# K products of a chunk in two groups, every other U of the first second stage in the ring of the spatial sums, and another order of the work

## The chip, the cores and the metric

The kernel runs on one core of a Trainium2 chip. A core has five engines, each with its own queue, which it works through in order: PE (TensorE, matmuls; its weight loads are shown apart as PEld), DVE (VectorE), ACT (ScalarE), POOL (GpSimd) and SP (SyncE, which here only issues transfers). The metric is the device time of one execution in microseconds (us). Before the change it is 365.99 us, the median of 8 runs (363.04 to 366.72).

## What is computed

Two branches work on the same input `x` of 2048 rows and 640 columns, and a gate mixes them:

```python
g = sigmoid((x * gate_w).sum(-1, keepdims=True))
# branch a: a long convolution along the rows, one filter of length 2048 per column
K = einsum('dn,dnl,dn->dl', C, exp(dt*A * l), dt*B).real      # d 640, n 128, l 2048
a = causal_convolution(K, x) + x * Dskip                       # by FFT in the reference
# branch b: a gated MLP with a product along the rows
z  = gelu(x @ w_in);  z1 = z[:, :864];  z2 = layernorm(z[:, 864:])
b  = (z1 * (w_sp @ z2 + b_sp[:, None])) @ w_out                # w_sp is 2048 x 2048
out = g * a + (1 - g) * b
```

All data are bf16; sums are kept in fp32.

## The kernel before

**Branch b.** `z2_tile` (matmuls at L606) makes z2, sixteen tiles of 128 rows. `z1_tile` (L638) makes z1 in four groups of rows and sends it to memory. `sp_block` is the product along the rows, in eight blocks `tb` of 256 output rows. In a block, 7 tiles of the 864 columns times 16 row tiles of z2 give 112 matmuls of 256 columns (L826, "spatial sums", into `ps_g`), 896 in all. They come in groups of two column tiles, so 32 matmuls fill one `ps_g` (the last group of a block has 16). VectorE adds the bias (L830) and multiplies by z1 (L832), which gives `vT`. Then 28 matmuls of 320 columns (L846, `ps_o`) multiply by `w_out`, 224 in all, and VectorE or ScalarE scales them into `ob` or, for the last four row tiles, `acc`.

**Branch a.** The filter K is made in eight chunks `c` of 80 columns; chunks 0 to 5 belong to the first part (`h` = 0, 480 columns), 6 and 7 to the second (`h` = 1, 160 columns). `k_tables` (L1001) makes tables of cosines, sines and exponentials in `ET`, kept twice, on VectorE, ScalarE and GpSimd. Its last step is the multiply at L1042. `k_sub` (L1048) multiplies the tables: 160 small matmuls a chunk (L1059 and L1060, 80 each, with 32 weight columns and 33 moving columns) into `ps_k`, a pair of PSUM banks. A copy moves it to `kf` (L1068, L1070). `k_store` sends kf to memory, `k_expand` reads it back spread out (`xk`). The convolution then goes by a transform in two stages. `s1_u` (L665, L669) is the first stage for the input, `conv_s1` (L1148, `ps_s1k`) that for the filter; both go through memory (`FU_d`, `FK_d`). `conv_s2` (L1169) is the second stage. For each of 32 indices k, a matmul makes U from `fu` (L1195, `ps_u`), ScalarE copies it to `us`, two matmuls make the filter's side from `fk` (L1202, `ps_s2k`), VectorE multiplies both into `p` (L1204), two matmuls transform back (L1210, `ps_v`), and ScalarE copies to `vs` (L1212). For the second part two indices are done at once, so there are 16 steps. `conv_vt` transposes `vs` on VectorE (L1218, twelve for the first part, four for the second), and `conv_i2` (L1290, L1292) is the last transform, added to branch b's result with the gate (L1226, L1243, L1245).

**PSUM.** Its eight banks are three rings: `two`, two pairs of banks, for `ps_z`, `ps_k`, `ps_s`, `ps_s1k`, `ps_s2k` and `ps_i`; `g`, two banks, for `ps_g` and for `ps_u` of the second part; `x`, two banks, for `ps_o`, `ps_v` and, in the first part, `ps_u`.

**What sets the order.** The program is a list of tasks, each with engines that may do it, a cost, what it reads and writes, and the rings it takes a buffer of. A planner (`Plan`, L139 to L331) plays the tasks through in time when the program is built: whenever an engine is free it takes, among its ready tasks with free buffers, the one with the longest chain of costs behind it plus a `bias`. Where a task may go to several engines, the one that is free takes it. The order so found is written out as the engines' queues. `TUNE` (L38) adds values to the bias of tasks named by function and line, some for one index only. A `lag` makes a task wait in the plan for some time after another; it makes no wait on the chip.

The lines that the change touches:

```python
        tab_ids.append(add("PE", 3.65, m, r=tabs + (["cva"] if h else []), w=[ps], bias=8000, lag=[(tab_ids[-1], 4.0)] if tab_ids else []))
        ...
        i_ = add(("ACT", "DVE"), (0.9, 0.91), ev, r=[ps], w=[(kf, s)], bias=8500)
        ...
            pu = gps("ps_u", [P, 512]) if h else xps("ps_u", [P, 512])
```

So the 160 matmuls of a chunk are one task, with nothing between them on TensorE.

Of the kernel before, what the change touches and what calls it, by code (L numbers as in the profile page):

```python
# [25 lines left out]
class Handle:  # L26
# [12 lines left out]
    ('conv_i2', 37, None): -4167,  # L39
    ('conv_s1', 15, ('g', 0)): -3985,  # L40
    ('conv_s1', 15, ('g', 1)): -4925,
    ('conv_s2', 35, ('h', 0)): 11440,
    ('conv_s2', 27, None): -2461,
    ('conv_s2', 10, None): 1034,
    ('conv_s2', 14, ('h', 0)): 1039,
    ('eights', 13, None): -327,
    ('i2_out', 7, None): -2142,
    ('k_expand', 28, None): -762,
    ('k_exps', 7, ('c', 0)): 1891,
    ('k_exps', 7, ('c', 4)): 2617,  # L50
    ('k_store', 13, ('h', 0)): -14806,
    ('k_store', 13, None): 22358,
    ('k_store', 14, ('h', 0)): 19878,
    ('k_store', 14, ('h', 1)): -1401,
    ('k_sub', 23, ('h', 1)): -10879,
    ('k_sub', 13, ('h', 0)): -8414,
    ('k_sub', 13, None): 1899,
    ('k_tables', 32, ('c', 3)): -2944,
    ('k_tables', 32, None): -581,
    ('k_tables', 41, None): 3697,  # L60
    ('k_tables', 30, ('c', 0)): -3593,
    ('k_tables', 30, ('c', 5)): -5856,
    ('k_tables', 29, None): -22708,
    ('k_tables', 6, ('c', 4)): 86,
    ('k_tables', 6, ('c', 5)): -857,
    ('k_tables', 18, ('c', 7)): 624,
    ('k_tables', 17, ('c', 6)): -17233,
    ('k_tables', 36, ('c', 0)): -6475,
    ('k_tables', 36, ('c', 5)): 223,
    ('k_tables', 36, ('c', 6)): -314,  # L70
    ('k_tables', 36, None): -460,
    ('k_tables', 20, None): -7652,
    ('k_tables', 21, ('c', 2)): 26183,
    ('k_tables', 21, ('c', 3)): 3768,
    ('k_tables', 21, None): -11620,
    ('main', 160, None): 8664,
    ('main', 151, ('g', 0)): 9963,
    ('main', 151, None): 1256,
    ('main', 149, None): 8266,
    ('main', 353, None): -19029,  # L80
    ('main', 370, None): -7683,
    ('main', 369, None): 304,
    ('main', 365, None): -1890,
    ('main', 438, None): 3692,
    ('main', 435, None): 82,
    ('main', 415, None): -970,
    ('main', 443, None): 5378,
    ('main', 421, None): 5294,
    ('main', 424, None): -198,
    ('ob_load', 7, None): 1449,  # L90
    ('quads', 6, None): -6309,
    ('s1_u', 13, ('h', 1)): 12507,
    ('s1_u', 13, ('n0', 12)): 8594,
    ('s1_u', 16, ('h', 1)): -18248,
    ('s1_u', 16, None): 3525,
    ('s1_u', 3, None): -3769,
    ('s1_u', 18, ('h', 1)): -8047,
    ('s1_u', 18, ('n0', 0)): 8453,
    ('s1_u', 14, ('h', 1)): -1860,
    ('s1_u', 14, ('n0', 6)): -9520,  # L100
    ('s1_u', 14, None): -5630,
    ('sp_block', 23, ('tb', 2)): 1896,
    ('sp_block', 23, ('tb', 7)): 872,
    ('sp_block', 25, None): 5230,
    ('sp_block', 20, ('tb', 0)): 7827,
    ('sp_block', 20, ('tb', 5)): -2187,
    ('sp_block', 20, ('tb', 6)): -2437,
    ('sp_block', 20, ('tb', 7)): -5504,
    ('sp_block', 20, None): -13871,
    ('sp_block', 41, None): 1955,  # L110
    ('sp_block', 42, ('tb', 0)): -7911,
    ('sp_block', 42, None): -1644,
    ('sp_block', 47, None): -33736,
    ('sp_block', 3, ('tb', 0)): 1637,
    ('sp_block', 3, ('tb', 4)): -553,
    ('sp_block', 8, ('tb', 0)): 580,
    ('sp_block', 8, ('tb', 1)): -2903,
    ('sp_block', 8, None): -115,
    ('sp_block', 6, ('tb', 0)): 8562,
    ('sp_block', 6, ('tb', 1)): 15972,  # L120
    ('sp_block', 6, None): -8530,
    ('sp_block', 5, ('tb', 7)): 4722,
    ('sp_block', 5, None): -667,
    ('tg_build', 15, None): 5531,
    ('tg_build', 9, None): 7974,
    ('x_group', 3, ('g', 0)): -1676,
    ('x_group', 3, ('g', 1)): -3059,
    ('z1_tile', 17, None): -290,
    ('z1_tile', 10, ('g', 0)): 3083,
    ('z1_tile', 10, ('g', 3)): -2857,  # L130
    ('z1_tile', 15, None): -1480,
    ('z2_tile', 19, None): 222,
    ('z2_tile', 18, None): 422,
    ('z2_tile', 10, None): -1879,
# [200 lines left out]
def kernel(  # L335
# [20 lines left out]
    P = 128  # L356
# [691 lines left out]
    def k_sub(h, s, kf):  # L1048
# [4 lines left out]
        def m(e):  # L1053
            ET, M2, E2 = X["ET", z], X["M2", z], X["E2", z]
            for i in range(SQ):
                for q in range(4):
                    d = SQ * q + i
                    o_ = ps()[32 * q:32 * q + 32, i // 10, 33 * (i % 10):33 * (i % 10) + 33]
                    pe.matmul(o_, lhsT=ET[:, 0:32, d], rhs=M2[:, :, d], start=True, stop=False, tile_position=(0, 32 * q))  # L1059
                    pe.matmul(o_, lhsT=ET[:, NA:NA + 32, d], rhs=E2[:, :, d], start=False, stop=True, tile_position=(0, 32 * q))  # L1060
        tab_ids.append(add("PE", 3.65, m, r=tabs + (["cva"] if h else []), w=[ps], bias=8000, lag=[(tab_ids[-1], 4.0)] if tab_ids else []))
# [327 lines left out]
```

## Time and profile before

| | us |
|---|---|
| median of 8 runs | 365.99 |
| the profiled execution, device time | 365.95 |
| its span, first to last instruction | 364.1 |
| TensorE busy | 316.0 |
| VectorE busy | 286.8 |
| ScalarE busy | 244.2 |
| GpSimd busy | 151.8 |

The mean clock that TensorE was granted is 0.947 of full speed. The span goes through these points: the first K chunk starts at 106.2 us and the eighth ends at 241.9; the first `ps_s2k` runs at 265.7; VectorE's transposes of the first part start at 312.6; the last instruction on VectorE is at 360.

How to read it: "busy" is the time in which an engine's instructions run, without waiting for one another. A timeline row gives start and length in us, engine, line, operation, output and inputs with their shapes, and how many instructions are merged; a bracket at its end is the time in which the engine sat idle before it, and what ended that. In a row of groups, the two numbers after the bar are busy us and mean ns of one; after the second bar stands the idle time of the engine just before the group's instructions, by releaser. The clock row (PEclk) has 40 slices of the span, each a digit in tenths, 9 for 0.9 and more.

### The profile page before, as it was taken

Reading aid. Unit: us, or ns where it says so; the run is one execution under the profiler, and the core shown is the slowest. Engines: PE = TensorE matmul, PEld = TensorE weight load, DVE = VectorE, ACT = ScalarE, POOL = GpSimd, SP = SyncE. Lnnn points to the kernel's source line nnn. Section 1 sums busy time; section 2 is a strip of 40 time slices with the busy share of each in tenths; the row PEclk is TensorE's granted clock in tenths of the full one; section 3 lists DMA queues with packets and bytes.
Section 4 is the critical chain, followed back from the end, with each engine's and each line's share of the span. In section 5 each row is a group of like instructions: output and inputs, shape, how many; then the busy total and the mean of one; then the engine's idle time right before and its main releaser. Section 6 shows DMA issues by size and latency. Waiting matters only on the chain.

```text
span 364.1 us, 8397 instructions
## 1 busy us (share of the span) xinstructions
PE 316.0 (87%) x3237; PEld 221.2 (61%) x3237; DVE 286.8 (79%) x548; ACT 244.2 (67%) x438; POOL 151.8 (42%) x143
## 2 busy tenths in 40 slices
PE   3899999997799999999798979879999999829963
PEld 3455455775485677787685668657755564516741
DVE  4059997887889589896898289727898989996984
ACT  1877757999785756899677368615467778605832
POOL 3004537600668068500899469826483000303111
PEclk9999999999899989999989899969999999967995
DMA  7989887585654569348395577977556767552403
GB/s 200 221 125 223 185 214 217 157 206 149 156 147 133 149 131 233 115 78 251 77 153 99 99 184 177 257 209 195 182 170 179 227 192 204 153 171 99 137 27 99
DMA packets 108085, 59.89 MB, mean 164 GB/s; under 512 B 75918, under 2 KB 104354, under 8 KB 108046
## 3 DMA queue, kind: packets, MB, share of 16 engines
q1 hardware_dynamic: 105662, 54.06, 59.2%
q0 software_dynamic: 2384, 5.30, 5.9%
q8 instruction: 25, 0.41, 0.5%
q14 instruction: 14, 0.11, 0.1%
HBM read 25.25 MB, written 19.47 MB: 123 GB/s over the span
## 4 chain that ended last, share of the span: by engine, by line
PE 24%; DVE 10%; POOL 8%; issue 4%; ACT 3%; DMA 1%; SPq 0%; POOLq 0%; DVEq 0%; ACTq 0%
PE ps_g L826 6%; POOL ci L375 6%; DVE vs L1218 5%; PE ps_v L1210 4%; PE ps_s2k L1202 4%; DVE p L1204 3%; PE ps_u L1195 2%; PE ps_s1k L1148 2%; PE ps_z L638 1%; PE ps_k L1059 1%; PE ps_o L846 1%; POOL xk L424 1%; PE ps_k L1060 1%; ACT ET L429 1%; ACT tm L1243 1%
## 5 line engine op out<-in xcount | busy, mean ns | idle before, releaser
L826 PE MATMUL ps_g<-wT,z2n 128*128 128x256 bf16 (+1 forms) x896 | 112.1, 279 | 11.7 <-DVE vT L830 11.2
L826 PEld LDWEIGHTS <-z2n 128*128 128x128 bf16 (+1 forms) x896 | 91.9, 104 | 32.0 <-issue 14.9
L375 POOL TENSOR_SCALAR ci<-ai 128x640 int32<-128x640 int32 (+1 forms) x12 | 34.8, 2915 | 54.7 <-ACT ET L429 28.3
L1204 DVE TENSOR_TENSOR p<-ps_s2k,us 128x960 bf16<-128x960 f32 (+1 forms) x48 | 48.4, 1040 | 4.7 <-ACT us L436 2.2
L846 PE MATMUL ps_o<-Wout,vT 128*128 128x320 bf16 (+1 forms) x224 | 35.4, 305 | 2.3 <-DVE ob L375 1.7
L429 ACT ACTIVATE ET<-ci 128x640 bf16<-128x640 int16 (+1 forms) x40 | 26.1, 678 | 15.8 <-POOL ci L375 13.7
L638 PE MATMUL ps_z<-xg,Win 128*128 128x512 bf16 (+1 forms) x140 | 33.3, 392 | 0.7 <-ACT gl L612 0.7
L1059 PE MATMUL ps_k<-ET 128*32 128x33 bf16 x640 | 28.2, 259 | 4.9 <-issue 3.2
L606 PE MATMUL ps_z<-Win,xT 128*128 128x432 bf16 (+1 forms) x160 | 31.0, 353 | 1.1 <-ACT gl L612 1.1
L1212 ACT CAST vs<-ps_v 128x480 bf16<-128x480 f32 (+1 forms) x48 | 24.6, 519 | 10.4 <-PE ps_v L1210 9.9
L1202 PE MATMUL ps_s2k<-fk,T 128*128 128x480 bf16 (+1 forms) x128 | 25.2, 309 | 7.1 <-DMA fk<-FK_d 6.1
L1059 PEld LDWEIGHTS <-ET 128*32 128x32 bf16 x640 | 27.3, 192 | 4.6 <-DVE ET L1042 3.0
L846 PEld LDWEIGHTS <-vT 128*128 128x128 bf16 (+1 forms) x224 | 21.9, 99 | 12.4 <-issue 3.0
L1060 PEld LDWEIGHTS <-ET 128*32 128x32 bf16 x640 | 27.5, 195 | 2.7 <-issue 2.5
L375 POOL TENSOR_SCALAR ci<-si 128x640 int32<-128x640 int32 x10 | 27.4, 2744 | 3.0 <-ACT ET L429 2.2
L1060 PE MATMUL ps_k<-ET 128*32 128x33 bf16 x640 | 28.2, 258 | 0.0
L1210 PE MATMUL ps_v<-p,G 128*128 128x480 bf16 (+1 forms) x128 | 25.2, 303 | 1.0 <-DVE p L1204 0.5
L424 POOL DMA_DIRECT2D FK_d<-s1k x10 | 8.4, 841 | 41.3 <-DVE s1k L436 36.2
L436 ACT CAST us<-ps_u 128x480 bf16<-128x480 f32 (+1 forms) x48 | 24.4, 518 | 1.7 <-PE ps_u L1195 1.1
L375 POOL TENSOR_SCALAR si<-th 128x80 int32<-128x80 f32 x32 | 22.3, 697 | 7.6 <-DVE ai L982 2.6
L429 ACT ACTIVATE mr<-lre 128x320 bf16<-128x320 f32 x66 | 25.0, 456 | 0.0
L606 PEld LDWEIGHTS <-xT 128*128 128x128 bf16 x160 | 15.7, 99 | 15.3 <-issue 2.4
(196 smaller groups left out, 620.1 us busy)
## 6 DMA issues: line engine op xcount, KB each, us to landing
FU_d<-s1u SPq DMA_DIRECT2D x16, 240.0 KB, 4.4
fu<-FU_d SPq DMA_DIRECT2D x16, 240.0 KB, 4.0
fk<-FK_d SPq DMA_DIRECT2D x16, 240.0 KB, 3.3
z_d<-zt SPq DMA_DIRECT2D x24, 128.0 KB, 2.0
z1t<-z_d SPq DMA_DIRECT2D x8, 384.0 KB, 5.1
FK_d<-s1k POOLq DMA_DIRECT2D x6, 480.0 KB, 4.8
xf<-in_A_u_dram SPq DMA_DIRECT2D x8, 320.0 KB, 4.3
Win<-in_B_w_in_dram SPq DMA_DIRECT2D x2, 1080.0 KB, 5.9
```

Source lines behind the costliest of these rows:

```text
L375: eng.tensor_scalar(out=out_, in0=in_, scalar1=s1, scalar2=None, op0=op0)
L429: return add("ACT", cost, lambda e: act.activation(out=out_(), in_=in_(), func=func, scale=scale), r=r, w=w, fset=fs, bias=bias, deps=deps ...
L606: pe.matmul(ps()[:, h, 0:432 + h], lhsT=xT[:, i, 128 * st:128 * st + 128], rhs=Win2[:, i, 432 * h:432 * h + 432 + h], start=(i == 0), stop ...
L638: pe.matmul(ps()[0:fs, ft - f0, :], lhsT=Win1[:, i, 128 * ft:128 * ft + fs], rhs=xg()[:, i, :], start=(i == 0), stop=(i == ND - 1))
L826: pe.matmul(ps()[0:fs, ft - f0, :], lhsT=z2n[:, st, 128 * ft:128 * ft + fs], rhs=wT()[:, st, :], start=(st == 0), stop=(st == NS - 1))
L846: pe.matmul(ps()[:], lhsT=vT[ft // 2]()[0:fs, ft % 2, 128 * r:128 * r + 128], rhs=Wout[0:fs, ft, HD * h:HD * h + HD], start=(ft == 0), sto ...
L1059: pe.matmul(o_, lhsT=ET[:, 0:32, d], rhs=M2[:, :, d], start=True, stop=False, tile_position=(0, 32 * q))
L1060: pe.matmul(o_, lhsT=ET[:, NA:NA + 32, d], rhs=E2[:, :, d], start=False, stop=True, tile_position=(0, 32 * q))
L1202: pe.matmul(ps()[:, i, W * n:W * n + W], lhsT=TK(k + n, i), rhs=fk()[:, j + n, :], start=True, stop=True)
L1204: add("DVE", dv1(2 * NW), lambda e, p12=p12, ps=ps, us=us: vec.tensor_tensor(out=p12()[:, :, 0:NW], in0=ps()[:, :, 0:NW], in1=us()[:, 0:NW ...
L1210: pe.matmul(pv()[:, W * n:W * n + W], lhsT=GV(k + n, i), rhs=p12()[:, i, W * n:W * n + W], start=(i == 0), stop=(i == 1))
L1212: add("ACT", 0.15 + NW / 1170, lambda e, k=k, pv=pv: act.copy(out=X["vs"][h][:, k:k + NK, :], in_=pv()[:, 0:NW].rearrange("p (k d) -> p k ...
```

## The change

Three things, in the order of the diff:

1. `TUNE` is replaced by another set of values, so the planner writes out another order, and gives some tasks to other engines.
2. The 160 K matmuls of a chunk become two tasks of 80, one for each of the two banks of `ps_k`. In the plan the second may start 1.3 us after the first, so other matmuls come between. The copy to kf reads both.
3. In the second stage of the first part, U of the odd indices takes its bank from ring `g`, that of the spatial sums, and not from ring `x`.

```diff
 TUNE = {
-    ('conv_i2', 37, None): -4167,
-    ('conv_s1', 15, ('g', 0)): -3985,
...
+    ('conv_s1', 18, ('g', 1)): 2327,
+    ('conv_s1', 18, None): -1981,
...
-        def m(e):
+        def m(e, hf):
             ET, M2, E2 = X["ET", z], X["M2", z], X["E2", z]
-            for i in range(SQ):
+            for i in range(SQ // 2 * hf, SQ // 2 * hf + SQ // 2):
                 for q in range(4):
...
-        tab_ids.append(add("PE", 3.65, m, r=tabs + (["cva"] if h else []), w=[ps], bias=8000, lag=[(tab_ids[-1], 4.0)] if tab_ids else []))
+        for hf in range(2):
+            tab_ids.append(add("PE", 1.85, lambda e, hf=hf: m(e, hf), r=tabs + (["cva"] if h else []), w=[(ps, hf)], bias=8000 + 500 * hf, lag=[(tab_ids[-1], 1.3 if hf else 4.0)] if tab_ids else []))
...
-        i_ = add(("ACT", "DVE"), (0.9, 0.91), ev, r=[ps], w=[(kf, s)], bias=8500)
+        i_ = add(("ACT", "DVE"), (0.9, 0.91), ev, r=[(ps, 0), (ps, 1)], w=[(kf, s)], bias=8500)
...
-            pu = gps("ps_u", [P, 512]) if h else xps("ps_u", [P, 512])
+            pu = gps("ps_u", [P, 512]) if h or k % 2 else xps("ps_u", [P, 512])
```

The values of `TUNE` say little by themselves; what they do is seen in the queues of the built programs. TensorE has the same matmuls in both. Matmuls that stand ahead of a point in its queue:

| ahead of | spatial sums before / after | ps_o | z1 | ps_s1k |
|---|---|---|---|---|
| first K chunk | 256 / 252 | 56 / 49 | 70 / 70 | 0 / 0 |
| fourth chunk | 508 / 448 | 112 / 84 | 105 / 105 | 0 / 0 |
| fifth chunk | 560 / 600 | 112 / 140 | 105 / 105 | 0 / 0 |
| sixth chunk | 564 / 616 | 140 / 140 | 125 / 135 | 0 / 0 |
| seventh chunk | 672 / 748 | 140 / 168 | 140 / 140 | 6 / 10 |
| eighth chunk | 688 / 784 | 168 / 168 | 140 / 140 | 16 / 16 |
| first ps_s2k | 804 / 896 | 196 / 196 | 140 / 140 | 32 / 32 |
| last ps_v of the first part | 896 / 896 | 203 / 224 | 140 / 140 | 38 / 34 |

After the change, all spatial sums thus stand ahead of the second stage; before, 92 stood in it. The two halves of the eighth chunk have 784 and 792 sums ahead of them.

Tasks that change engines: of the 40 steps `ci` of the tables VectorE has 26 (before 18) and GpSimd 14 (before 22). Of the 16 steps `si` (L1015) VectorE has 10 (before 12), and GpSimd 6, eight instructions each (before 4). Of the 32 copies `s1u` VectorE has 8 (before 14) and ScalarE 24 (before 18). The first copy M2 at L1007 is on GpSimd four times (before once) and on VectorE twice (before five times). Of the stores to FK_d, GpSimd issues 6 and SP 6 (before 10 and 2); of the loads xk, GpSimd issues 25 and SP 29 (before 19 and 35).

## The prediction

> **What bounds the kernel now.** I read the page's busy shares and clock row first, then the busy time of each engine by stage, then TensorE's timeline at the clock's dips, then the groups of the second stage.
>
> ```profile
> PE 316.0 (87%) x3237; PEld 221.2 (61%) x3237; DVE 286.8 (79%) x548; ACT 244.2 (67%) x438; POOL 151.8 (42%) x143
> PEclk9999999999899989999989899969999999967995
> ```
>
> No engine is full. The clock row shows dips at about 95, 127, 182, 204, 243 and 320 us. The stage view (stretch, length, then busy us of PE, PEld, DVE, ACT, POOL, clock, DMA share, GB/s) says who bounds what:
>
> ```profile
> 203.00:242.00 39.00, 33.35 (x504) 25.59 (x503) 23.75 (x48) 22.60 (x35) 25.12 (x20) 0.94 0.78 194
> 242.00:266.00 24.00, 23.31 (x166) 17.20 (x166) 18.32 (x38) 12.49 (x15) 13.37 (x15) 0.90 0.62 177
> 266.00:313.00 47.00, 46.60 (x279) 26.54 (x278) 43.56 (x49) 36.08 (x69) 11.05 (x17) 1.00 0.63 181
> 313.00:364.00 51.00, 32.02 (x260) 22.42 (x257) 40.68 (x57) 21.77 (x52) 9.05 (x10) 0.82 0.39 116
> ```
>
> Up to 242 us (end of the eighth K chunk) TensorE waits here and there: from 110 to 242 the same view gives 118.2 us busy of 132, so 13.8 us idle. From 242 to 313 it is full. After 313 it waits for VectorE's transposes, and VectorE bounds the rest.
>
> TensorE's timeline (start, length, group; the bracket is idle time before it and its releaser) shows two prices of a K chunk:
>
> ```profile
> 126.25 0.28 PE L1059 MATMUL ps_k<-ET 128*32 128x33 bf16 x4
> ...
> 127.86 0.98 PE L665 MATMUL ps_s<-xf,F 128*128 128x480 bf16 x2
> 128.64 5.62 PE L826 MATMUL ps_g<-wT,z2n 128*128 128x256 bf16 x40
> ...
> 207.62 6.71 PE L826 MATMUL ps_g<-wT,z2n 128*128 128x256 bf16 x60
> ...
> 241.30 0.30 PE L1059 MATMUL ps_k<-ET 128*32 128x33 bf16 x4 [2.42 <-issue]
> ```
>
> 40 spatial sums take 5.62 us right after a chunk, where 60 take 6.71 later: the clock is halved from 127.7 to 130.6 though TensorE hardly paused. In 1 us windows the clock missing there adds up to 1.7 us; after the chunk of 199.4 us (cold 202.8 to 206) it is 1.7 again. In the eighth chunk TensorE stops for 2.42 us with no releaser ("issue"), and then cold until 246.5: 2.8 us more. K chunks thus cost about 1.7 + 1.7 + 2.4 + 2.8 = 8.6 us beyond their own 8 x 3.54 us. Idle waits (2.55 us before 95.9, 2.53 before 182.2, both on VectorE's vT) cost two more cold spells of 1.7.
>
> [...] the spells above last about 3.3 us at clock 0.50. That a chunk of 128x32 weights counts as idle [...] is my reading of the 127.7 and 202.8 spells, where hardly any idle time precedes them. [...] A chunk has 320 (160 matmuls and as many weight loads), and DMA share was 1.02 in 230 to 240 us. [...]
>
> **The change, part by part.** No instruction is added on TensorE or taken away: 3237 matmuls either way.
>
> (1) *K in two groups.* Between the two halves 1.3 to 2.2 us of dense matmuls now run (ten z1 matmuls at 0.216 at most, eight sums and two ps_s1k at least). The spells after chunks go: 1.7 + 1.7, and I count the stall and what of its spell falls before 242 (2.4 + 0.3) as gone too: 6.1. The gain is bounded below by zero (halves throttle too, and the stall comes elsewhere) and above by these 6.1. The copy kf (0.44 + 0.43 us) comes later by the matmuls between the halves, and their PSUM pair is held as much longer; z1 and ps_s1k use the other pair meanwhile. The next chunk's tables are kept twice, so this is covered; without that cover each chunk would pay up to 2.2 us.
>
> (2) *Order up to the eighth chunk.* I count the PE work queued before a point with rates of the timeline: spatial sum 0.109 us, ps_o 0.136, z1 0.216, z2 0.188, K 3.54 a chunk, 480 columns 0.205. To the end of the eighth chunk that was 200.7 us; in the new order it is 212.4, as 792 spatial sums stand before it and not 688. It ended at 241.9, so 41.2 us were not work. If no other idle is filled: 241.9 + 11.7 - 6.1 = 247.5. If the added sums fill all the other idle of 110 to 242 (13.8 - 2.4 = 11.4): 236.1. VectorE's rows before the last table multiply (L1042) sum to 211.6 us against 213.0, ScalarE's before its last table sine to 180.1 against 179.2, GpSimd loses 8 of 22 ci (2.7 to 3.3 us each) and gains 16 si rows (0.70 each). So the tables don't come later in sum; but ScalarE's work before the first sine tables is 2.2 us longer, with s1u copies (0.96) moved to it. I take three tenths of the idle filled, as the sums themselves wait for VectorE: 247.5 - 3.4 = **244.1**.
>
> (3) *From there to the first ps_s2k.* Before 23.8 us: 20.3 of work, 2.4 of cold clock, 1.1 else. Now 18.6 of work (104 sums 11.3, 28 ps_o 3.8, 14 ps_s1k 2.9, three U 0.6). The other path: last ps_s1k of the first part 10.8 us after the chunk, then copy, FK_d, and fk, which took from 256.3 to 264.0 in the trace, 7.7 us: 18.5. Both are due together; with 1.2 of waiting, as before, **19.8**: 263.9. FK_d stores move from GpSimd's queue to SP's (6 of 12 there, not 2) and six xk loads the other way, at 0.35 to 0.84 us an issue; fk stands behind FK_d in SP's queue and needs it anyway.
>
> (4) *The first second stage.* 92 of the 896 spatial sums lay in it (10.0 us of the 46.6); now none does. TensorE's work is 32 x 5 x 0.205 = 32.8 plus 28 ps_o, 3.8: 36.6. VectorE becomes the bound:
>
> ```profile
> L1204 DVE TENSOR_TENSOR p<-ps_s2k,us 128x960 bf16<-128x960 f32 x32 | 35.9, 1151 | 3.2 <-ACT us L436 2.2 <-PE ps_s2k L1202 0.7
> L1212 ACT CAST vs<-ps_v 128x480 bf16<-128x480 f32 x32 | 17.8, 565 | 8.8 <-PE ps_v L1210 8.8
> ```
>
> Back to back a p takes 1.05 to 1.10 us (two in 2.20 at 266.52); at 1.08 that is 34.6 for 32. Rows that stay in the stage are three G at 0.6, two ti at 0.4, two acc at 0.46, a kg: 3.8, and two s1k copies 1.5: 39.9. ScalarE's two copies (vs and us, 0.56 each) stay just below an index of 1.13. How near it can come is set by the rings:
>
> ```profile
> 305.78 0.56 PE L1202 MATMUL ps_s2k<-fk,T 128*128 128x480 bf16 x2
> ...
> 307.01 0.57 PE L1202 MATMUL ps_s2k<-fk,T 128*128 128x480 bf16 x2
> 308.22 0.57 PE L1202 MATMUL ps_s2k<-fk,T 128*128 128x480 bf16 x2
> ```
>
> With no sum between, an index took 1.22 us, with U and V sharing two banks, more than the 1.03 of TensorE and the 1.08 of VectorE. With odd U's in the other ring I take 1.13, between 1.08 and 1.22, for 24 indices: 24 x 0.05 = 1.2 more, and 1.2 to start: **42.3** against 46.9 (265.7 to 312.6). Bounds 39.9 and 46.9. fu and fk must bring 0.246 MB an index, 217 GB/s at 1.13; the page had slices of 251 and 257.
>
> (5) *The tail.* Transposes, 16 narrower p's and the outputs: VectorE's list has the same transposes, p's and L1226 rows, and 7 adds against 9. Before 51.5 us (312.6 to 364.1); now the same, plus or minus 1.5. The 21 ps_o that ran beside the transposes are now earlier, counted in (4); their cover, VectorE's 40 us there, holds.
>
> Sum: 244.1 + 19.8 + 42.3 + 51.5 = 357.7 of span. The profiled run took 365.95 with a span of 364.1, so 1.85 lies around it: **359.6** us. Its time is that of the median, 365.99, within 0.1.
>
> **Rivals.**
> *A, forecast:* as above, 356 to 362.5. For it: TensorE full from 242, work taken from there, cold spells that follow chunks.
> *B, slower:* the 104 sums put ahead of the last chunk meet vT's that stand behind table rows in VectorE's queue, and the K halves wait behind them on TensorE. Such waits cost 2.1 to 2.6 us at 95.9, 182.2 and 216.5, and two of these brought a cold spell: 4.2 each. For it: VectorE is in order and 184.2 us busy of the first 242 already. Against: its sum before the last table falls by 1.4. It ends slower from the second such wait on: 359.6 + 8.4 = 368.0.
> *C, little changes:* the stage keeps its 46.9 us, as fu and fk are three buffers deep and land in 3 to 4 us: 359.6 + 4.6 = 364.2, and 367.6 if nothing of the idle is filled either. Against: 181 GB/s in that stage now, 289 elsewhere.
> *D, the split doesn't do what it says:* halves with 1.3 us between still count as idle. Then 1.7 + 1.7 come back: 363.0.
>
> **From this to the numbers.** A 0.52, D 0.12, C 0.14, B 0.22. The measurement can tell about 0.5%, 1.8 us, from no change. A and D are faster by more; C is within; B slower. So 0.64, 0.14, 0.22. Range 354 (idle filled well, and the stage at its lower bound in part) to 368.5 (C whole, and B with two waits); the likeliest case alone 356 to 362.5.
>
> **What would show it.** (1): no clock of 0.5 right after a K half without an idle wait; no "issue" gap in a chunk. (2): the last ps_k ending at 240 to 248. (3): the first ps_s2k 19 to 21 us later. (4): VectorE over 40 us busy in a stage of 41 to 44, TensorE near 37. (5): 50 to 53 us from the first transpose to the end. The forecast is wrong if the last chunk ends after 250, or the stage stays at 46 or more.

## The result, and the profile after

The changed kernel took 362.02 us (median of 18 runs, 359.75 to 364.63) against 364.75 for the kernel before (53 runs): ratio 0.993, 95% interval 0.991 to 0.995. A second set gave 362.72 against 365.31, ratio 0.994 (0.991 to 0.996). By the medians the change gains 2.6 to 2.7 us; the forecast was 6.4. The measured time lies inside the stated range of 354 to 368.5 us, 2.4 us above the forecast of 359.6.

Busy shares and granted clock of the changed kernel's profiled run, from its page:

```profile
span 357.9 us, 8414 instructions
PE 310.1 (87%) x3237; PEld 215.4 (60%) x3237; DVE 281.0 (79%) x547; ACT 246.0 (69%) x440; POOL 148.2 (41%) x160
PEclk9999999999999999999999999899999999987997
```

Of the dips ahead of 300 us one is left, at 227 us. Its stages, with the columns of the stage view of before (stretch, length, then busy us of PE, PEld, DVE, ACT, POOL, clock, DMA share, GB/s):

```profile
203.00:248.50 45.50, 40.19 (x669) 32.55 (x665) 30.01 (x60) 21.73 (x33) 22.41 (x23) 0.96 0.75 167
248.50:267.80 19.30, 18.92 (x151) 14.61 (x150) 12.94 (x26) 11.07 (x14) 11.07 (x14) 1.00 0.81 219
267.80:310.10 42.30, 40.36 (x199) 18.37 (x197) 41.36 (x49) 35.51 (x70) 13.93 (x20) 1.00 0.70 200
310.10:357.90 47.80, 28.92 (x248) 20.05 (x247) 40.47 (x56) 22.06 (x51) 10.32 (x11) 0.89 0.42 125
```

The eighth K chunk ends at 248.5 us, not 242. The stretch after it is 4.4 us shorter than the 23.7 of before, the first second stage takes 42.3 (VectorE busy 41.4 of it, as forecast), the tail 47.8. What holds the chunk back is in TensorE's timeline (start, length, group, idle time and its releaser) and in POOL's:

```profile
219.75 3.22 PE L804 MATMUL ps_g<-wT,z2n 128*128 128x256 bf16 x28
227.58 1.65 PE L1127 MATMUL ps_s1k<-xk,F 128*128 128x480 bf16 x4 [4.61 <-DMA xk<-KA_d]
229.02 2.51 PE L804 MATMUL ps_g<-wT,z2n 128*128 128x256 bf16 x12
```

```profile
216.03 6.74 POOL L353 TENSOR_SCALAR ci<-si 128x640 int32<-128x640 int32 x1 [0.67 <-ACT ET L407]
222.72 4.46 POOL L402 DMA_DIRECT2D xk<-KA_d  x8
```

TensorE waits 4.61 us for xk, eight of whose loads stand on POOL behind a conversion of 6.74 us. It then runs cold, which here means at a granted clock of 0.50: the trace records that from 227.7 to 231.1 us, and 12 sums take 2.51 us, where 28 had taken 3.22.

One more profile of each kernel shows what belongs to the kernel and what to one execution (experiments 1 and 2):

| us | before, 1st | 2nd | after, 1st | 2nd |
|---|---|---|---|---|
| end of the eighth K chunk | 242.0 | 241.5 | 248.5 | 249.8 |
| to the first ps_s2k | 23.7 | 23.4 | 19.3 | 19.3 |
| to the first transpose | 46.9 | 46.6 | 42.3 | 42.8 |
| to the end | 51.5 | 51.5 | 47.8 | 47.8 |
| span | 364.1 | 363.0 | 357.9 | 359.7 |
| median span of all runs seen | 363.5 (79) | | 360.25 (38) | |

The first profile of after was the fastest of its 38 runs, 2.35 us under the median span, while the first of before lay 0.6 above. So the two first profiles overstate the change by 3 us. The second pair is 3.3 apart, as the median spans are (3.25); I use it below. The times differ by less, 2.6 to 2.7, in part because the changed kernel has more time outside its span, a median of 2.1 us against 1.8 in the second set; nothing here shows why.

### The profile page after: what moved, and what is told of

It reads as the page before. It is cut to its first block, busy times and chain, and to the rows that moved or that the text cites. A ratio compares the mean times of both kernels' runs of the same rounds, so it can differ in the third digit from the quotient of the medians.

```text
span 357.9 us, 8414 instructions
## 1 busy us (share of the span) xinstructions
PE 310.1 (87%) x3237; PEld 215.4 (60%) x3237; DVE 281.0 (79%) x547; ACT 246.0 (69%) x440; POOL 148.2 (41%) x160
## 4 chain that ended last, share of the span: by engine, by line
DVE 34%; PE 33%; ACT 11%; DMA 8%; issue 7%; SPq 3%; POOL 3%; ACTq 0%; DVEq 0%; POOLq 0%
PE ps_g L804 8%; DVE p L1183 5%; DVE vs L1197 5%; PE ps_z L616 4%; PE ps_o L824 3%; PE ps_s2k L1181 3%; DMA FU_d<-s1u 3%; PE ps_v L1189 3%; PE ps_k L1037 3%; DMA xk<-KA_d 3%; PE ps_s1k L1127 2%; PE ps_k L1038 2%; PE ps_z L584 2%; POOL ci L353 2%; ACT mr L407 2%
## 5 line engine op out<-in xcount | busy, mean ns | idle before, releaser
L804 PE MATMUL ps_g<-wT,z2n 128*128 128x256 bf16 (+1 forms) x896 | 106.8, 274 | 7.3 <-DVE vT L808 6.8
L804 PEld LDWEIGHTS <-z2n 128*128 128x128 bf16 (+1 forms) x896 | 88.9, 102 | 22.8 <-issue 9.1
L353 POOL TENSOR_SCALAR si<-th 128x80 int32<-128x80 f32 x48 | 40.2, 837 | 20.6 <-DVE t3p L753 8.1
L824 PE MATMUL ps_o<-Wout,vT 128*128 128x320 bf16 (+1 forms) x224 | 33.8, 299 | 1.6 <-ACT ob L828 1.6
L616 PE MATMUL ps_z<-xg,Win 128*128 128x512 bf16 (+1 forms) x140 | 32.2, 380 | 1.8 <-ACT zt L407 1.5
L407 ACT ACTIVATE ET<-ci 128x640 bf16<-128x640 int16 (+1 forms) x40 | 26.5, 679 | 9.3 <-POOL ci L353 5.3
L1037 PE MATMUL ps_k<-ET 128*32 128x33 bf16 x640 | 28.9, 260 | 1.2 <-DVE ET L1020 0.5
L353 POOL TENSOR_SCALAR ci<-ai 128x640 int32<-128x640 int32 (+1 forms) x5 | 13.1, 2622 | 38.0 <-ACT s1u L414 26.9
L1038 PE MATMUL ps_k<-ET 128*32 128x33 bf16 x640 | 28.5, 258 | 0.0
L808 DVE TENSOR_TENSOR vT<-ps_g,br 128x512 bf16<-128x512 f32 (+1 forms) x32 | 18.6, 616 | 11.8 <-PE ps_g L804 11.8
L414 ACT CAST s1k<-ps_s1k 128x960 bf16<-128x960 f32 (+1 forms) x16 | 13.3, 859 | 19.6 <-PE ps_s1k L1127 19.4
```

Of the source, the lines that this page charges most:

```text
L353: eng.tensor_scalar(out=out_, in0=in_, scalar1=s1, scalar2=None, op0=op0)
L407: return add("ACT", cost, lambda e: act.activation(out=out_(), in_=in_(), func=func, scale=scale), r=r, w=w, fset=fs, bias=bias, deps=deps ...
L414: (vec.tensor_copy if e == "DVE" else act.copy)(out=out_(), in_=in_())
L616: pe.matmul(ps()[0:fs, ft - f0, :], lhsT=Win1[:, i, 128 * ft:128 * ft + fs], rhs=xg()[:, i, :], start=(i == 0), stop=(i == ND - 1))
L804: pe.matmul(ps()[0:fs, ft - f0, :], lhsT=z2n[:, st, 128 * ft:128 * ft + fs], rhs=wT()[:, st, :], start=(st == 0), stop=(st == NS - 1))
L824: pe.matmul(ps()[:], lhsT=vT[ft // 2]()[0:fs, ft % 2, 128 * r:128 * r + 128], rhs=Wout[0:fs, ft, HD * h:HD * h + HD], start=(ft == 0), sto ...
```

## The experiments

Times are medians, each with its ratio to the kernel before, measured on the same chip. The bracket has the 95% interval. Each run has one profile. Nothing of the computation is left out in any of them.

**1 and 2: both kernels again, unchanged.** No edit.

> The kernel before, unchanged, profiled once more. The first profile of it lost 19.3 us of full clock in sum, in spells that began in the K chunks among others, and stood 1.2 us above the median of its runs. Theory ([...] one profile is one draw): the median stays within 0.3% of 364.8 us, but the second profile has other spells, at least one of the two after whole K chunks gone or a new one elsewhere, the sum of lost clock differs by 3 us or more, and the span follows it. Rival (the first profile is typical): the same spells at the same places, lost clock 18 to 20.5, span 363.5 to 364.6.

> The changed kernel, unchanged, profiled once more. Theory: the wait of TensorE for xk ahead of the first ps_s1k is made by the new order, so it is there again with 4 to 5.5 us, followed by a cold spell, and the eighth K chunk ends at 247 to 250 us; no cold spell follows the K halves; but the tail after the first transpose, 47.8 us in the first profile, is 49 to 52 [...], and the span lies 2 us above the first profile's 357.9. Rival (the wait for xk is an accident of that execution): under 2 us, eighth K chunk at 244 to 245, span below 357.

The kernel before took 365.33 us, ratio 0.999 (0.997 to 1.002), span 363.0. The draw was another, as expected. The pause called issue is there again (3.02 us in the eighth chunk), and the cold spell with it; the spells of 96 and 127 us are gone, those of 182 and 202 are not. Lost clock, the share of the clock that was not granted times the span, fell from 19.3 to 16.0 us. The changed kernel took 362.72; the wait for xk is 4.66 us, the chunk ends at 249.8, the tail is 47.8, not 49 to 52. So the wait belongs to the new order, and the short tail is no luck, against what I had expected; of the 1.8 us by which the first profile was faster, 1.3 lie ahead of the chunk's end.

**3: whole K chunks in the new order.** All 160 matmuls of a chunk are issued where its second half stood.

```diff
-            for i in range(SQ // 2 * hf, SQ // 2 * hf + SQ // 2):
+            ps()
+            for i in range(SQ if hf else 0):
```

> The changed kernel with its order kept on every engine, but the 160 matmul pairs of a K chunk issued in one piece where the second half stood. Theory (the split by itself takes the cold spells and the pause in issuing away): spells of 1.7 us come back after one to three of the eight chunks, the lost clock grows by 2 to 6 us, and the time by 1.5 to 5 us over the changed kernel (363.5 to 367). Rival (the order did it, the split does nothing): within 0.8 us of the changed kernel, 361.2 to 362.8, with no spell after the chunks.

This took 366.02 us, ratio 1.002 (1.000 to 1.005), which is 3.3 us over the changed kernel, but not for the reason given. The chunk ends at 249.3, no later than in experiment 2; no cold spell follows the first seven whole chunks. All of the loss is after the eighth (part of it in the tail, 49.2 us against 47.8). There TensorE's timeline has

```profile
249.25 0.39 PE L804 MATMUL ps_g<-wT,z2n 128*128 128x256 bf16 x2
252.50 0.39 PE L804 MATMUL ps_g<-wT,z2n 128*128 128x256 bf16 x2 [2.86 <-issue]
252.73 0.57 PE L824 MATMUL ps_o<-Wout,vT 128*128 128x320 bf16 x3
```

a pause without a releaser and 1.7 us of lost clock after it: 24.0 us to the first ps_s2k, not 19.3.

**4 and 9: every other U back in the ring x.** In 4 the planner then makes another order from the first ps_u on; in 9 every queue is kept row for row and only the bank differs. The first edit is that of 4, the second that of 9.

```diff
-            pu = gps("ps_u", [P, 512]) if h or k % 2 else xps("ps_u", [P, 512])
+            pu = gps("ps_u", [P, 512]) if h else xps("ps_u", [P, 512])
```

```diff
+            pu = gps("ps_u", [P, 512]) if h else Handle("g", lambda: psX.tile([P, 512], F32, name="ps_u", tag="x")) if k % 2 else xps("ps_u", [P, 512])
```

> The changed kernel with every other ps_u of the first second stage put back in the ring x; the queues are the same up to the first ps_u. Theory (the ring of the spatial sums gives the second stage its room): the stretch from the first ps_s2k to the first transpose goes from 42.3 back to 45 to 47 us, and the time rises by 2 to 4.6 us (364 to 366.6). Rival (the order of the stage did it, and the ring is no matter): the stretch is 42 to 43.5 us and the time within 0.8 us of the changed kernel's 362.0. Third case (the start of the tail hides part): the stretch grows by 2 us or more but the time by under 1.5.

> The changed kernel with every queue kept row for row, and only the bank of every other ps_u of the first second stage taken from the ring x instead of the ring of the spatial sums. In the earlier run with U back in x the planner had also made another order from the first ps_u on. Theory (the ring itself makes the room): stage 47 to 50 us instead of 42.5, and the time 4.5 to 8 us over the changed kernel (367 to 370.5), the tail keeping its 47.8 us. Rival (most of the 9.6 us was the other order): stage 43 to 45, time 363 to 365.5.

Experiment 4 took 372.17 us, ratio 1.020 (1.014 to 1.026), with a stage of 48.9 us and a tail of 51.8. Experiment 9 took 363.82 us, ratio 1.000 (0.997 to 1.003), beside 0.993 for the changed kernel; its stage, from these two rows of TensorE and VectorE, takes 45.76 us:

```profile
266.96 0.98 PE L1181 MATMUL ps_s2k<-fk,T 128*128 128x480 bf16 x4
```

```profile
312.72 2.48 DVE L1197 STREAM_TRANSPOSE vs<-vs 128x640 f32<-128x640 f32 x2
```

The truth lies between the two cases, near the rival: the ring itself is worth 3.0 us of the stage and 0.7% of the time, 2.4 us; the rest of the 9.5 in experiment 4 was the other order. The tail stays 48.1 in 9, so the ring has no part in it.

**5 and 6: each edit alone in the order of before.** In 5, six of the eight chunks are issued in two halves with following matmuls of at least 1.3 us by the planner's costs, where that many were free, pulled between; in 6 the planner orders what follows the first U.

```diff
+            if i in self.halves:
+                self.halves[i](0)
+                got, c = self.ahead(order, p, 1.3, left, slot, gone)
+                for j, x in got:
+                    emit(j, x)
             emit(i, e)
...
-            for i in range(SQ):
+            for i in range(SQ // 2 * hf, SQ // 2 * hf + SQ // 2):
```

```diff
-            pu = gps("ps_u", [P, 512]) if h else xps("ps_u", [P, 512])
+            pu = gps("ps_u", [P, 512]) if h or k % 2 else xps("ps_u", [P, 512])
```

> The kernel before with its order kept, but six of its eight K chunks issued in two halves with a few of the matmuls that followed them pulled in between (the first and the sixth chunk stay whole); DVE, ACT, POOL and SP have the same queues as before. Theory (the split by itself is worth about 3 us, as undoing it in the changed kernel cost): the pause in issuing of 2.4 to 3.0 us at the eighth chunk and the cold spell after it go, the lost clock falls by 3 to 8 us, and the time by 2 to 4.5 us (360.8 to 363.3). Rival (in the order of before the next wait absorbs it, on vT or on the copies of s1k): within 1 us of 365.3, with the waits of TensorE longer by what the pause was.

> The kernel before with every other ps_u of the first second stage in the ring of the spatial sums, the rest of its order as its own planner then makes it, without a searched order for it. Theory (the ring is worth 6.6 us in the stage and 4 us in the tail, as taking it away from the changed kernel cost): stage 46.7 to 40 to 43, tail 51.5 to 47.5 to 50, time lower by 4 to 9 us (356 to 361). Rival (the ring gains only where the order was searched for it, and what was lost without it is the loss of any order that was not searched): time between 363.5 and 372, the stage 45 us or more.

Experiment 5 took 367.81 us, ratio 1.006 (1.004 to 1.008), slower. The pause is still there (1.85 us), there are cold spells too, and the eighth chunk ends at 244.7, three us later; the likely reason, which no run here isolates, is that the pulled work delays the ends of the chunks, and kf with them. Experiment 6 took 371.21 us, ratio 1.014 (1.010 to 1.018), with a stage of 51.9. In the order of before neither edit gains. Experiment 6 cannot tell the ring from the unsearched order; the same bank with the queues of before kept was not run.

**7 and 8: the wait for xk.** In 7 POOL issues eight xk loads ahead of ci<-si; in 8 the 12 sums between the first two groups of ps_s1k go ahead of the first.

```diff
+            if p == first:
+                for j, x in xp:
+                    emit(j, x)
```

```diff
+            if i in self.late:
+                got, c = self.ahead(order, p, self.late[i], left, slot, gone, set(self.late))
+                for j, x in got:
+                    emit(j, x)
```

> The changed kernel with one move: the first eight loads of xk on POOL stand ahead of the conversion ci<-si instead of behind it; all other queues are the same. Theory (this conversion, 6.74 us long on POOL, is what TensorE waits for through xk): the wait ahead of the first ps_s1k falls from 4.7 to 0 to 1.5 us, the cold spell after it goes, the eighth K chunk ends 3 to 6 us earlier, and the time falls by 3 to 5.5 us against the changed kernel (357 to 359.5). Rival (the loads on SP or the stores before them land as late): the wait stays over 3 us and the time within 1 us of 362.5. Third case (the conversion is now late for the next ET): the wait goes, but the seventh or eighth K chunk waits for ET instead and the time changes by under 1.5 us.

> The changed kernel with one move on TensorE: the 12 ps_g matmuls that stood between the first and the second group of ps_s1k go ahead of the first; all other queues are the same. Theory (the wait for xk ends by the loads, whatever TensorE does before it): the wait shrinks by the 1.4 us of the moved matmuls to 3 to 3.5 us, the first ps_s1k starts at the same time, the work after it is shorter by that, and the time falls by 0.5 to 1.5 us (361 to 362.1). Rival (the copies of s1k and the FK stores behind them set what follows, so matmuls moved ahead save nothing): within 0.4 us of 362.5.

Experiment 7 took 362.45 us, ratio 0.987 (0.982 to 0.993; six runs, spans 357.2 to 363.4), not the 357 to 359.5 expected. The first part went as expected, TensorE waiting 1.09 us and no spell following:

```profile
226.15 0.97 PE L1177 MATMUL ps_s1k<-xk,F 128*128 128x480 bf16 x4 [1.09 <-DMA xk<-KA_d]
...
230.18 1.11 PE L1177 MATMUL ps_s1k<-xk,F 128*128 128x480 bf16 x4 [1.74 <-DVE s1k L464]
...
250.40 0.61 PE L854 MATMUL ps_g<-wT,z2n 128*128 128x256 bf16 x2 [2.39 <-issue]
```

But a wait of 1.74 for a copy comes next. The chunk ends at 247.7, 2.1 earlier than in experiment 2; this execution was 1.3 us behind before the moved loads came, and counted from the end of the sixth chunk the eighth ends 3.5 earlier (2.9 against the first profile of after). Then the pause of experiment 3 stands there, although the chunk was halved. In the profiled run, at 362.4 among the slower of the six, this took the gain back. Experiment 8 took 362.04 us, ratio 0.989 (0.984 to 0.993; four runs). The wait fell to 2.94, and counted from the sixth chunk the eighth ended 1.2 us earlier than in experiment 2 (0.7 against the first profile). Its time agrees with the theory's 361 to 362.1 by little and does not settle it.

**What the pauses have in common.** The DMA view of the kernel before has this queue (packets, MB, share of 16 engines):

```profile
q8 instruction: 25, 0.41, 0.5%
```

In the first trace of each kernel every one of these 25 packets has 16384 bytes. From the first packet to the last, TensorE's records (3237 matmuls and as many weight loads) go from 181 to 6319 in before and from 191 to 6305 in after, over 24 packets: 255.8 and 254.8 a packet. That a packet brings 256 of TensorE's instructions is my reading of these counts and of the queue's name; I call it a fetch. I counted TensorE's records up to each pause: 5035 in the first profile of before, 5283 in experiment 3, 5290 in 7. From 5035 to 5290 is once 256, a record aside; I call such a count a boundary. In all three a packet of that queue is recorded within 0.2 us of the pause's start, and TensorE resumes 2.3 to 2.7 us after it; in the first profile of after, which has no such pause, the packet ran when 5109 were counted, 181 ahead of that boundary. In experiment 3, from 247.5 to 251.5 us, around the pause, the DMA view has

```profile
DMA packets 1312, 1.50 MB, mean 374 GB/s; under 512 B 77, under 2 KB 1311, under 8 KB 1311
## 3 DMA queue, kind: packets, MB, share of 16 engines
q1 hardware_dynamic: 1296, 1.48, 106.0%
q8 instruction: 1, 0.02, 1.7%
```

The 16 DMA engines are full (the share of q1 is 106.0%). Two loads wT<-ob_d of 480 KB and three fu<-FU_d of 240 KB had just been issued on SP.

**10, 11, 12: 1.4 MB out of the way.** The two wT<-ob_d loads go behind the last fk load of the first part, the second and third fu behind the KA_d stores of the eighth chunk; 11 adds the edit of 7, 12 that of 3.

```diff
+            if i in kept and kept[i] not in gone:
+                last[kept[i]].append((i, e))
+                continue
...
+            for j, x in last.get(i, ()):
+                emit(j, x)
...
+pl.grp[0][0].extend([fi] if h == 0 and k in (2, 4) else [])
...
+pl.grp[1][0].extend([oi] if a < 8 else [])
```

> The changed kernel with one move on SP: two loads wT<-ob_d of 480 KB (needed in the tail only) go far back, and the second and third load fu<-FU_d of 240 KB behind the KA_d stores of the eighth K chunk, so that 1.4 MB less are under way when TensorE's own instructions are fetched near 245 to 250 us; all other queues are kept. Theory (the pause called issue is a fetch of 16 KB of TensorE's instructions that stands behind data on the DMA engines, and comes in some executions of the changed kernel, in others not): no pause in the profile, the runs above 362 become rare, and the median falls by 0.7 to 2 us (360.5 to 361.8). Rival (the pause has to do with the K matmuls alone): no change of the median beyond 0.5 us and the same spread of 6 us.

> Both moves together: eight loads of xk ahead of ci<-si on POOL, and the 1.4 MB of later loads out of the way on SP. Theory (the shorter wait for xk gained 2 to 3 us, which a pause of 2.4 us and its cold spell took back in the profile with the first move alone): wait for xk 1 us, no pause, eighth K chunk at 245 to 247.7, gap to the first ps_s2k 19 to 20, span 356 to 358.5, median 358 to 360. Rival (the work after the K chunk is bound elsewhere, and the move of the loads makes ps_u late): the gap stays 22 to 24 us and the time at 361.5 to 363.

> The changed kernel with whole K chunks, as in the earlier run that showed a pause of 2.86 us after the eighth, and the same 1.4 MB of loads out of the way. Theory (the pause is made by the loads that stand ahead of the instruction fetch, the whole chunk only runs out of instructions sooner): the pause is gone or under 1 us, the gap from the eighth chunk to the first ps_s2k falls from 24.0 to 19.5 to 21, time 362 to 364. Rival (320 matmuls in one piece use their instructions up faster than they can be fetched, whatever else moves): the pause of 2 to 3 us stays, time 365 to 366.5.

Experiment 10 took 361.61 us, ratio 0.993 (0.991 to 0.996), no different from the changed kernel, as the rival had it: that kernel has no such pause in its two profiles to take away. Experiment 11 took 358.57 us, ratio 0.985 (0.982 to 0.989). TensorE waits 0.59 us for xk and, at a later ps_s1k, 2.25; there is no pause, and 19.3 us pass to the first ps_s2k; the chunk ends at 248.1, later than expected. Experiment 12 took 361.72 us, ratio 0.994 (0.991 to 0.997): with whole chunks as in 3, and these loads elsewhere, the time is that of 10. Its DMA view in the same 4 us, and TensorE's timeline:

```profile
DMA packets 205, 0.03 MB, mean 8 GB/s; under 512 B 204, under 2 KB 204, under 8 KB 204
## 3 DMA queue, kind: packets, MB, share of 16 engines
q1 hardware_dynamic: 204, 0.02, 3.6%
q8 instruction: 1, 0.02, 2.0%
```

```profile
248.30 0.27 PE L1105 MATMUL ps_k<-ET 128*32 128x33 bf16 x4
248.50 0.61 PE L870 MATMUL ps_g<-wT,z2n 128*128 128x256 bf16 x4
248.95 1.12 PE L890 MATMUL ps_o<-Wout,vT 128*128 128x320 bf16 x7
```

There is no pause: the packet that in 3 ran at 249.8 us runs here at 246.1, in the chunk (the one in the view is that of the next 256 records). Between 3 and 12 only four loads moved, two wT and two fu. In this order, then, the pause comes with the transfers ahead of the fetch and goes with them, in the profiles (2.86 us and none) and in the medians (366.02 and 361.72 us).

**13 and 16: the pause of the kernel before.** In 13 its first three fu loads go behind the KA_d stores, in 16 two FK_d stores of 480 KB as well.

```diff
+pl.grp[0][0].extend([fi] if h == 0 and k in (0, 2, 4) else [])
```

```diff
+pl.grp[0][0].extend([i_] if h == 0 and 2 * g + ab in (2, 3) else [])
```

> The kernel before with one move on SP: the first three loads fu<-FU_d (720 KB in all), issued at 235.3 us beside 1.44 MB of FK_d stores and just as the eighth K chunk begins, go behind the KA_d stores of that chunk; all else is kept. Theory (the pause of 2.4 to 3.7 us in the eighth chunk is an instruction fetch behind that traffic; 720 KB take 1.9 us at 380 GB/s): the pause shrinks by 1 to 2.5 us or goes, the cold spell after it shortens, the stretch to the first ps_s2k ends 2 to 4 us earlier, time 361.5 to 363.5. Rival (the pause is owed to the whole K chunk): the pause stays 2.4 us or more, time 364 to 365.5, or later if ps_u now waits for fu.

> The kernel before with the fu loads late as in the last run of it, and two of the three FK_d stores (480 KB each) that POOL issues at 232 to 235.6 us moved behind the KA_d and first KB_d store of the eighth K chunk; whole chunks, all other queues kept. With the fu loads alone moved, the DMA engines stayed full from 235.0 to 238.4 us, the fetch packet ran at 237.5 to 238 and the pause stayed 2.83 us. Theory (whatever is ahead of the fetch packet makes the pause): the packet runs by 236.5, the pause falls under 1.5 us or goes, the gap from the eighth chunk to the first ps_s2k falls from 23.4 to 19.5 to 21.5 us; the time to 361 to 364, unless the ring of s1k now waits for the moved stores and takes part of it back. Rival (in the order of before the whole chunk makes the pause by itself): the pause is still 2.4 us or more with the engines free.

Experiment 13 took 365.99 us, ratio 1.002 (1.000 to 1.005): the pause is 2.83 us, and the rival holds as to the time. Experiment 16 took 372.27 us, ratio 1.012 (1.008 to 1.017), since ps_s1k waits for a copy, which itself waits 8.56 us for one of the moved stores to leave its buffer:

```profile
242.31 0.29 PE L1125 MATMUL ps_k<-ET 128*32 128x33 bf16 x4 [1.98 <-issue]
...
254.54 0.96 PE L1214 MATMUL ps_s1k<-xk,F 128*128 128x480 bf16 x2 [5.51 <-ACT s1k L502]
```

The pause is at the same boundary (5029 records in both) and shrinks with the traffic, 2.83 to 1.98, but stays. In each profile below the packet for the boundary ran 0.3 to 4.6 us after the record that stands 256 ahead of it. From that record, in us (records that are missing from a trace can shift these by about 0.1):

| profiles | chunk | DMA share meanwhile | to the packet | to the boundary | pause |
|---|---|---|---|---|---|
| 12, 15 | whole | under 0.1 | 0.3, 0.5 | 2.9 | none |
| 3 | whole | 1.0 | 3.4 | 2.9 | 2.86 |
| both of before, 13 | whole | 1.0 | 3.1 to 3.7 | 2.7 | 2.42, 3.02, 2.83 |
| 16 | whole | 0.6 | 2.6 | 2.7 | 1.98 |
| both of after | halves | 1.0 | 1.0, 1.4 | 4.2 | none |
| 7 | halves | 1.0 | 4.6 | 4.4 | 2.39 |

In a whole chunk TensorE uses up 96 records a us, so 256 records last 2.7 to 2.9 us; with halves and the matmuls between them they last 4.2 to 4.4. An estimate from this table: a packet as early as in 12 and 15, and 2.3 to 2.8 us to resume, would leave the whole chunk of before a pause of at most about 0.6 us. So most of the 1.98 in 16 is the packet's delay of 2.6; that the traffic left (0.17 to 0.28 MB a us from 237 to 239.5 us) made this delay is likely and not shown.

**14 and 15: both moves again, with halves and with whole chunks.** No edit against 11; that of 3 in 15.

> The version with both moves, unchanged, once more, since its median came from six runs. Theory: median 357.8 to 359.2, no pause, gap from the eighth chunk to the first ps_s2k 19.3 us. Rival (a draw of fortunate runs): 359.5 to 361, in line with each move alone.

> The version with both moves, but with whole K chunks. Theory (once nothing stands ahead of the fetch, the split is worth nothing): within 0.8 us of the version with both moves and halves (358 to 359.5), no spell that follows a whole chunk without idle time before it, gap 19.3 us. Rival (a whole chunk uses its instructions up faster than they come, by itself): a pause of 1 to 3 us is back and the time at 360 to 362.5.

Experiment 14 took 360.27 us, ratio 0.986 (0.981 to 0.990), as in 11 on a chip on which before is 0.9 us slower. Experiment 15 took 361.16 us, ratio 0.988 (0.985 to 0.992). The 0.9 us between them is within the intervals; there is no pause over 0.5 us in either. The version with both moves is faster than both kernels of the case, and by 1.5% faster than the one before.

## Why the forecast was wrong, step by step

Measured from the second profile of before to the second of after, in us:

| step | forecast | measured |
|---|---|---|
| (1), (2) end of the eighth chunk | +2.2 | +8.3 |
| (3) to the first ps_s2k | -4.0 | -4.1 |
| (4) first second stage | -4.6 | -3.8 |
| (5) tail | 0 | -3.7 |
| sum | -6.4 | -3.3 |

**Steps (1) and (2) failed.** The eighth chunk ended 6.1 us later than they have it, measured from one kernel to the other. The forecast took three spells or pauses off (6.1) and let three tenths of the other idle time be filled.

The *spells*: the forecast's estimate that a chunk of 128x32 weights counts as idle, so that the chunk itself brings the spell and halves take it away, does not hold. Experiments 12 and 15 have whole chunks, and no spell follows any of the sixteen. The starts of all spells of one profile lie whole multiples of 3.413 us apart: in the first of before they come at 96.73, 127.46, 182.07, 202.55, 240.10, 322.01 and 356.15 us, which is 9, 16, 6, 11, 24 and 10 times that from one to the next. All but the last, which runs to the end of the record, have a length of 3.41, 6.83 or 10.24 us at a granted clock of 0.50. So windows of 3.413 us, counted from those starts, can be laid over each trace and compared, from 50 to 300 us in the 18 profiles:

| K matmuls in the window, us | idle TensorE in the window, us | spell after it |
|---|---|---|
| none | under 1.83 | never |
| none | 1.83 to 1.97 | four of nine times |
| none | over 1.97 | always |
| 2 or more | under 0.05 | never in 53 |
| 3.17 | 0.24 | yes at 202 us in before, no at 204 us in 16 |
| 2.72 | 0.70 | yes, at 127 us in before |

Without K matmuls a little over half of a window idle was enough: in the first of before 2.42 us idle in the window from 178.7 us were followed by a spell, 1.87 in that from 212.8 were not. Beside a chunk far less was enough, 0.24 and 0.70 us in the table. Counting K matmuls as half idle, with a limit of 1.91 us, sorts all but 6 of 1272 windows that began at full clock; counting them as busy or as wholly idle leaves at least 15 or 46 on the wrong side. So a chunk, by this estimate from the windows, counts about half: too little for a spell alone, enough for one with a short wait. The two spells that the forecast counted had such waits, which I had passed over: 1.39 us for zt, begun in the window before, and a pause of 0.80 in the second chunk, which ended 2.4 us after an instruction packet; pause and spell were both gone in the second profile. Up to the eighth chunk the cold clock that fell on work went from about 3.5 to 2.25 us, not down by 3.7.

So TensorE's *busy time* to the chunk's end rose by 13.1 us (210.3 to 223.3), not by the 8.0 that the forecast has (11.7 of work less 3.7 of cold clock). 2.4 of the 5.1 are the spells. Another 1.3 to 1.6 are the halves themselves, whose price the forecast left at that of a whole chunk: up to the end of the eighth chunk the K matmuls are busy 30.3 us in experiment 2 and 28.7 with whole chunks in 3, 12 and 15. About 1 us is work that my rates put too low, not told apart by row.

The *idle time* fell by 4.8 us (31.3 to 26.5), not by 5.8. That looks near, but the 26.5 hold a wait that the forecast lacked, 4.66 us for xk; the others fell by 9.4. The forecast saw six xk loads move to POOL and priced their issues; it did not price the row they stand behind, nor count that only 15.0 us of work were left between the sixth chunk and the first ps_s1k, when kf took 20.4 us through memory to xk (16.8 in 7, with the loads first). What the wait alone costs is less than its length: in 14 it is 0.62, then a copy of s1k is waited for, 2.23 us, and the chunk ends 3.6 us earlier, counted from the sixth chunk (3.1 against the first profile of after).

The *pause* did go, as forecast. The forecast had no mechanism for this; the traces show its fetch 1.0 and 1.4 us after the record 256 ahead, with 4.2 us from that record to the boundary. Experiment 3 puts the split at 3.3 us with the loads where the change has them, 12 and 15 at 0 to 1 with the loads elsewhere, and 7 shows the pause with halves. The split leaves a late fetch more time, 4.2 to 4.4 us for 256 records and not 2.7 to 2.9; it is neither needed (12, 15) nor enough (7).

**Step (3) held**, 19.3 against 19.8.

**Step (4) held**: VectorE bounds the stage, and 9 puts the ring's part at 3.0 of the 3.8. The shares differ from the forecast: at its own rates the stage would take 39.9 + 24 x 0.14 + 1.2 = 44.5 us with all U in the ring x (1.22 an index), where 9 has 45.8, so the ring brought more and taking the 92 sums away less. From the page's groups in the stage, VectorE's wait ahead of p fell from 3.2 us to

```profile
L1183 DVE TENSOR_TENSOR p<-ps_s2k,us 128x960 bf16<-128x960 f32 x32 | 35.4, 1151 | 0.6 <-ACT vs L1191 0.4 <-ACT us L414 0.2
```

**Step (5) missed a gain** of 3.7. It was put at nothing because VectorE's list there was the same; by luck its error hid more than half of the one above. The stretch in before and in after:

```profile
312.60:364.10 51.50, 32.41 (x263) 22.71 (x260) 41.08 (x58) 22.17 (x52) 9.05 (x10) 0.82 0.39 115
```

```profile
310.10:357.90 47.80, 28.92 (x248) 20.05 (x247) 40.47 (x56) 22.06 (x51) 10.32 (x11) 0.89 0.42 125
```

VectorE's list is nearly the same length (41.1 and 40.5); it is idle for 7.3 us in place of 10.4, of which 3.6 and 3.8 lie after its last row. In after the first of the narrow p's stand between the outputs, nine back to back after them, and two fewer additions wait for ScalarE's tm. I had counted the rows and not what they wait for. This is read off the queues, and no experiment tests it; experiment 9 shows only that it isn't the ring.

The rivals: B's waits for vT came to 6.8 us, down from 11.2, so it was not they; its shape, a new wait with a cold spell that gives the gain back, was right with xk in the place of vT. C is out, as the stage took 42.3 us. D is out as put: no spell follows a half, but none follows a whole chunk without idle time beside it either.

Last, the anchor. The sum was made against one profile 0.6 us over the median span. With 1.85 us taken off for what lies around the span, the forecast meant a span of 357.7, which is the changed kernel's best run and not its typical 360.25.

## What to carry to other kernels

When an order is changed, price the row ahead of each moved DMA issue, and count the work left between a store and the load that reads it back. Here a whole chunk of small matmuls went through 256 of TensorE's records in 2.7 us, and where the packet of the instruction queue came 3.1 us after the record 256 ahead, TensorE stood still for 2.42: look for the packets of that queue beside a pause called issue, and keep big loads that nobody needs yet away from them (366.02 us in 3, 361.72 in 12). Look for the idle time behind a cold spell before blaming the work alone; beside 2.72 us of K matmuls in a window 0.70 us of idle time was enough here.

## What was not expected of the hardware

The granted clock fell to 0.50 on short waits: in the 18 profiles idle time of over 1.97 us in a window of 3.413 without K matmuls was always followed by a cold spell, and counting the 128x32 matmuls as half idle, an estimate, sorts all but 6 of 1272 windows. TensorE stood still for 2.86 us in experiment 3, where a packet of the instruction queue, 16 KB, ran within 0.2 us of the pause's start while data filled the DMA engines (106.0%); in 12, with four loads moved on SP, there was no pause, and 4.7 us were gone from the middle of the span (24.0 to 19.3). Pauses of 2.42, 2.83 and 1.98 us stood after 5035, 5029 and 5029 records in the first profile of before and in 13 and 16, which have its order. And the conversion ci<-si, 128x640, took 6.74 us on POOL ahead of the loads in after, 1.82 when it came behind them in experiments 7 and 14; spans on POOL are rough. VectorE was busy in 5.1 of the 6.74 us and idle throughout the 1.82; no run tests whether that is the reason.
